# Block-sparse attention followed by a Fourier-mixing MLP: key sums read first, second weight by casting DMA, second-product pieces moved past the norm, exponentials and causal selects over two PSUM banks

## Chip, cores, metric

One core of one Trainium2 chip runs the whole program. The metric is device microseconds (us) of one execution, lower is better. Each experiment ran its kernel and the kernel before on the same chip in the same session, and a verdict uses the runs of the fast state alone. For a single core that state only tells runs within 1.5% of the fastest from slower ones, and it is judged within a session: a run that counts as fast in one session can count as slow in another.

## The reference

The inputs are q, k, v of shape (4, 8, 768, 64) and two weights, (512, 2048) and (2048, 512), all float32. The output is (4, 768, 512).

```python
# attention: 12 key blocks of 64; each query keeps its own block and the 3 best causal blocks
k_rep = k.reshape(B, H, 12, 64, D).mean(axis=3)
gate  = where(causal_block, q @ k_rep^T, -1e9);  top_idx = argsort(gate)[..., -3:]
attn  = softmax(mask(top_idx or own block, causal)(q k^T / 8)) @ v        # (4, 8, 768, 64)
x     = attn with the heads side by side                                 # (4, 768, 512)
# MLP
u   = x + real(fft(fft(x, axis=1), axis=2))
un  = (u - mean(u)) / sqrt(var(u) + 1e-6)                                 # over the 512 features
out = u + relu(un @ w1) @ w2
```

## The kernel before

The eight heads of a batch are four pairs, so there are 16 pairs. A pair goes through four stages in four consecutive slots: A (transposes of q and k, key sums), B (gate), D (scores, exponentials, causal selects), V (times v). The MLP of batch b runs between the attention of batch b+1, piece by piece: a list of generators is interleaved by the cost that each piece states. So a piece's place in the program, not its readiness, decides when TensorE comes to it: in the trace of this kernel the last fold (`fg`) of batch 3 is done at 265.7 us, and TensorE takes up its first matmul on the folds at 286.4 us, behind eight second-product pieces (279.5 to 286.4 us) that stand before it in the program. That is what "in order" means. Batch 0's attention has no MLP beside it, and the last MLP has no attention beside it.

Names used below: `tp` transposes, `kr` key sums, `gtp`/`g`/`gmp` gate matmul, its transpose and the resulting mask, `sc` scores, `ptl` exponentials, `av` attention output, `sd`, `zw`, `fg` folds of x by symmetry, `yp` and `mx` the two Fourier matmuls, `ha`/`hb` the first product (512 and 256 columns), `ch` the second product.

Stage A: ScalarE copies a bank of transposed keys, then VectorE sums it per block (four such banks a pair, two of them keys).

```python
for who in range(2):                       # 0: q, 1: k
    for g in range(2):
        ps = pst([128, 3, 128], f"tp_{hp}_{who}_{g}")
        ...  # three TensorE transposes
        if who == 0:
            nc.vector.tensor_copy(out=qt[:, cols], in_=flat)
        else:
            nc.scalar.copy(out=kI[0][0:64, cols], in_=flat[0:64])
            nc.scalar.copy(out=kI[1][0:64, cols], in_=flat[64:128])
            nc.vector.tensor_reduce(out=kr12[:, 6 * g:6 * g + 6], in_=..., op=add)
...
for e in range(2):                         # query copies, on GpSimd
    nc.gpsimd.tensor_scalar(out=qg[e][0:64, :], in0=qt[64 * e:64 * e + 64, :], ...)
```

Stage D: six PSUM banks of scores per head, one exponential each; the bank holding diagonal blocks gets a causal select on GpSimd.

```python
for bi, bank in enumerate(BANKS):          # 5 banks of 512 columns, 1 of 128
    for e in range(2):
        sp = pst([128, wid_bank], ..., tag="sc", bufs=3)      # 5 general banks + 3 of these
        ...  # matmuls
        nc.scalar.activation(out=pt[:, po:po + wid_bank], in_=sp, func=AF.Exp, scale=0.125)
        if ndiag:
            nc.gpsimd.affine_select(out=dg, in_=dg, ...)
```

Weights: sixteen loads of 0.5 MB into float32 staging (issued by SyncE), sixteen float32-to-float16 casts on GpSimd.

```python
W_LOAD = {1: ('fft', 0, 1, 2, 3), 3: (4, 5, 6, 7), 5: (8, 9, 10, 11), 7: (12, 13, 14, 15)}
W_CAST = {3: (0, 1, 2, 3), 5: (4, 5, 6, 7), 7: (8, 9, 10, 11), 9: (12, 13, 14, 15)}
def emit_weight_cast(c): nc.gpsimd.tensor_scalar(out=dst, in0=wst[c], ...)
```

MLP of batch b, with the 24 pieces (four matmuls, 0.86 us each) of the second product of batch b-1 as filler `w2(n)`:

```python
tt(fg..., ADD);  yield from w2(2)
tt(fg..., SUB);  yield from w2(1)
tt(fg..., SUB);  yield from w2(1)
tt(fg..., ADD);  yield from w2(4)
...  # yp: first Fourier matmul, copies
for hf in range(2):
    ...  # mx: second Fourier matmul, u, statistics
    yield from w2(4)
    ...  # normalise three row tiles, DMA-transpose them into unT
    yield from w2(2)
yield from w2(100)                         # what is left
...  # first product (ha, hb) from unT
```

The softmax here doesn't subtract the row's maximum and nothing guards it: scores larger than these inputs give would overflow.

## Time and profile before

| | before |
|---|---|
| time | 363.17 us, median of 3 (362.57 to 363.66) |
| profiled execution, span | 358.5 us |
| TensorE clock, mean over the span | 0.94 |

The table of busy time by stretches of 20 us. Each line gives the stretch, its length, then busy us and instructions for TensorE (PE), its weight loads (PEld), VectorE (DVE), ScalarE (ACT), GpSimd (POOL), then the granted TensorE clock, the mean DMA share, and GB/s.

```profile
core 0: us, PE busy (x) PEld busy (x) DVE busy (x) ACT busy (x) POOL busy (x), PEclk, DMA share, GB/s
20.00:40.00 20.00, 17.22 (x174) 11.97 (x169) 12.54 (x50) 15.62 (x36) 12.77 (x21) 0.91 1.11 236
40.00:60.00 20.00, 16.31 (x188) 11.75 (x186) 16.50 (x57) 15.32 (x34) 17.96 (x24) 0.91 1.23 234
60.00:80.00 20.00, 16.35 (x174) 11.58 (x173) 19.25 (x60) 13.84 (x31) 14.52 (x18) 0.91 1.11 237
80.00:100.00 20.00, 14.80 (x167) 10.21 (x166) 19.31 (x52) 11.31 (x27) 12.60 (x17) 0.85 0.88 169
100.00:120.00 20.00, 19.38 (x151) 11.86 (x151) 15.03 (x48) 11.40 (x24) 6.89 (x10) 0.73 0.59 101
...
200.00:220.00 20.00, 20.00 (x175) 12.54 (x173) 13.36 (x47) 12.50 (x26) 5.05 (x8) 1.00 0.16 12
...
300.00:320.00 20.00, 16.36 (x75) 7.84 (x74) 7.88 (x18) 2.84 (x5) 1.11 (x2) 0.83 0.28 73
```

From 120 to 300 us TensorE is 95 to 100% busy at full clock. From 20 to 100 us no engine is the limit alone; VectorE comes nearest at 60 to 100 and GpSimd at 40 to 60. A closer look, in stretches of 4 us, at the end of that stage:

```profile
84.00:88.00 4.00, 4.00 (x40) 3.24 (x38) 4.00 (x11) 3.31 (x7) 2.58 (x5) 1.00 1.51 203
88.00:92.00 4.00, 2.91 (x39) 2.17 (x37) 4.00 (x19) 3.86 (x10) 3.80 (x6) 1.00 0.37 74
92.00:96.00 4.00, 0.92 (x21) 0.81 (x21) 4.00 (x6) 0.00 (x0) 3.84 (x5) 0.73 0.60 61
96.00:100.00 4.00, 3.02 (x18) 1.42 (x18) 4.00 (x12) 0.37 (x1) 0.48 (x1) 0.50 0.90 132
100.00:104.00 4.00, 3.68 (x24) 3.04 (x24) 3.75 (x11) 1.65 (x4) 1.17 (x3) 0.50 0.99 204
104.00:108.00 4.00, 4.00 (x15) 1.54 (x14) 3.97 (x20) 3.90 (x8) 2.94 (x5) 0.50 0.41 80
```

At 92 to 96 us VectorE has no free moment and TensorE works 0.92 us; the clock is 0.50 from 93.9 us, for 17.1 us. What VectorE and GpSimd did there, from the timeline (start, length, engine, line, operation, output and inputs):

```profile
90.86 1.97 DVE L324 SCALAR_TENSOR_TENSOR gmp_1550<-gsb_1548,other_75 128x144 f16<-128x144 f32 x1
```

```profile
90.66 0.91 POOL L230 DMA_DIRECT2D v_all<-in_v_dram  x1
91.61 1.06 POOL L201 TENSOR_SCALAR w_sb<-wst_1220 128x1024 f16<-128x1024 f32 x1
```

`gmp` takes 1.97 us here and 0.30 elsewhere (23.93 and 33.59 us, for instance). It ends just after GpSimd's cast does.

In the view of waits (who waited for whom: us in total, times, longest), VectorE's key sums wait for ScalarE's copies of the same bank; the two lines add up to 15.5 us over the whole run:

```profile
DVE kr_1_78 L282 <- ACT kI_all L281: 10.2, 9, 2.2
...
DVE kr_0_77 L282 <- ACT kI_all L281: 5.3, 6, 1.9
```

The end of the run, from the timeline; the bracket gives idle time and what ended it. The last second-product pieces of batch 2 run out at 306.5 us:

```profile
305.59 1.03 PE L572 MATMUL ch_5_4621<-w_sb,hT_2_3_4147 128*128 128x512 f16 x4
...
307.48 0.38 PE L559 MATMUL ha_0_4644<-unT_4491,w_sb 128*128 128x512 f16 x1 [0.87 <-DVE u_3464 L576]
...
310.63 0.37 PE L560 MATMUL hb_0_4645<-unT_4491,w_sb 128*128 128x256 f16 x1 [2.77 <-DMA unT_4491<-x_3666]
...
310.80 0.63 PE L559 MATMUL ha_0_4644<-unT_4491,w_sb 128*128 128x512 f16 x1
...
311.44 0.63 PE L559 MATMUL ha_0_4644<-unT_4491,w_sb 128*128 128x512 f16 x1
```

TensorE stands still for 0.87 and 2.77 us and then needs 0.63 us for a matmul that takes 0.38 at full clock (the granted clock is 0.50 from 308.9 us, for 6.8 us).

### The profile page before, as it was taken

The numbers are of one execution on the slowest core, as the hardware profiler recorded it, in microseconds if no ns is written. First come the engines' busy times: TensorE is split into PE (matmuls) and PEld (weight loads), VectorE is DVE, ScalarE is ACT, GpSimd is POOL, SyncE is SP. The second block draws the span as 40 slices with busy tenths as digits, with TensorE's granted clock in tenths as the row PEclk, the third lists the DMA queues.
The fourth block names the chain that finished last, engine by engine and source line by source line (L and its number), as shares of the span: only waits on it lengthen the run. The fifth ranks groups of instructions, "written<-read, shape, count | busy, mean of one in ns | idle before, by whom it ended". The sixth has DMA issues, their size and how long they took to land.

```text
span 358.5 us, 7035 instructions
## 1 busy us (share of the span) xinstructions
PE 323.4 (90%) x2650; PEld 197.5 (55%) x2650; DVE 227.7 (64%) x690; ACT 175.8 (49%) x363; POOL 117.9 (33%) x174
## 2 busy tenths in 40 slices
PE   5678978699499999999899999999999999599995
PEld 2346656467355665656466665656565555256442
DVE  1564987999995765579857576499673167323121
ACT  1497767578264764647266854733634130034100
POOL 2574988686743410315332312141300002000000
PEclk9698989999758999999999999999999999789999
DMA  9999999989565350354923030013300003300012
GB/s 184 181 155 276 260 274 184 299 201 259 68 142 94 56 68 0 101 71 97 148 73 24 4 22 32 31 45 60 103 2 2 29 32 102 103 2 0 29 69 79
DMA packets 96154, 35.47 MB, mean 99 GB/s; under 512 B 89224, under 2 KB 89704, under 8 KB 96120
## 3 DMA queue, kind: packets, MB, share of 16 engines
q1 hardware_dynamic: 66296, 30.65, 34.2%
q0 software_dynamic: 25120, 3.18, 14.4%
q10 hardware_dynamic: 4704, 1.18, 2.1%
q8 instruction: 21, 0.34, 0.4%
q14 instruction: 13, 0.11, 0.1%
HBM read 28.71 MB, written 6.29 MB: 98 GB/s over the span
## 4 chain that ended last, share of the span: by engine, by line
PE 63%; DVE 19%; ACT 12%; DMA 3%; issue 2%; POOL 0%; SPq 0%; ACTq 0%; DVEq 0%; POOLq 0%
ACT kI_all L281 2%; DMA qn_103<-in_q_dram 2%; ACT kI_all L280 2%; DVE sd_596 L452 1%; DVE kr_0_77 L282 1%; PE warm L129 1%; PE ch_0_3470 L572 1%; PE ch_0_2295 L572 1%; PE ch_2_3773 L572 1%; DVE x_1358 L546 1%; PE ch_5_4931 L572 1%; PE ch_5_4621 L572 1%; PE ch_5_4081 L572 1%; PE ch_4_3981 L572 1%; PE ch_2_4874 L572 1%
## 5 line engine op out<-in xcount | busy, mean ns | idle before, releaser
L354 PEld LDWEIGHTS <-kI_all 76*128 76x128 f16 x416 | 33.2, 102 | 19.7 <-issue 4.4
L559 PEld LDWEIGHTS <-w_sb 128*128 128x128 f16 x256 | 25.6, 100 | 30.4 <-issue 4.3
L230 POOL DMA_DIRECT2D v_all<-in_v_dram x32 | 27.5, 861 | 30.0 <-PE av_0_1873 L386 4.8
L560 PEld LDWEIGHTS <-w_sb 128*128 128x128 f16 x256 | 25.4, 100 | 8.4 <-issue 4.9
L540 POOL TENSOR_SCALAR rstd_3_4493<-stat_3_4492 128x3 f32<-128x3 f32 x2 | 0.5, 234 | 46.8 <-DVE stat_3_4492 L537 46.8
L561 ACT ACTIVATE hT_3_0_4640<-ha_0_4644 128x512 f16<-128x512 f32 x1 | 0.6, 597 | 22.3 <-issue 22.3
L129 PE MATMUL warm<-warm_src 128*128 128x512 f16 x26 | 11.4, 438 | 0.0
L540 POOL TENSOR_SCALAR rstd_2_3705<-stat_2_3704 128x3 f32<-128x3 f32 x2 | 0.5, 235 | 18.5 <-DVE stat_2_3704 L537 18.5
L452 DVE TENSOR_TENSOR sd_596<-x_543 128x384 f16<-128x384 f16 x8 | 5.1, 654 | 0.1
L129 PEld LDWEIGHTS <-warm_src 128*128 128x128 f16 x26 | 2.8, 106 | 3.7 <-issue 3.4
L142 PE MATMUL warmps<-warm_src 128*128 128x512 f16 x8 | 3.6, 631 | 1.3 <-DVE kr_1_78 L149 1.3
L546 DVE TENSOR_SCALAR x_543<-u_1198,stat_0_1478,rstd_0_1479 128x512 f16<-128x512 f32 x6 | 4.5, 805 | 0.2 <-POOL rstd_0_1479 L542 0.2
L546 DVE TENSOR_SCALAR x_3666<-u_4394,stat_3_4492,rstd_3_4493 128x512 f16<-128x512 f32 x6 | 2.9, 543 | 2.6 <-POOL rstd_3_4493 L542 2.6
L365 POOL TENSOR_SCALAR_AFFINE_SELECT ptl_0_2318<-ptl_0_2318 128x512 f16<-128x512 f16 (+1 forms) x2 | 1.0, 520 | 10.7 <-ACT ptl_0_2318 L361 10.7
L546 DVE TENSOR_SCALAR x_1358<-u_2289,stat_1_2535,rstd_1_2536 128x512 f16<-128x512 f32 x6 | 3.8, 671 | 0.8 <-POOL rstd_1_2536 L542 0.8
L560 PE MATMUL hb_0_4645<-unT_4491,w_sb 128*128 128x256 f16 x4 | 1.6, 406 | 2.8 <-DMA unT_4491<-x_3666 2.8
L304 ACT COPY gts_1729<-gtp_1725 96x256 f32<-96x256 f32 x1 | 0.4, 368 | 7.4 <-PE gtp_1725 L301 7.4
L508 ACT CAST yg_0_4448<-yp_0_4441 128x386 f16<-128x386 f32 x1 | 0.6, 599 | 6.9 <-PE yp_0_4441 L497 6.9
L562 DVE TENSOR_SCALAR hT_3_0_4640<-hb_0_4645 128x256 f16<-128x256 f32 x1 | 0.4, 424 | 5.6 <-PE hb_0_4645 L560 5.6
L572 PEld LDWEIGHTS <-hT_3_1_4641 128*128 128x128 f16 x24 | 2.3, 98 | 2.8
L572 PEld LDWEIGHTS <-hT_3_2_4642 128*128 128x128 f16 x24 | 2.3, 98 | 2.8
L572 PEld LDWEIGHTS <-hT_3_3_4643 128*128 128x128 f16 x24 | 2.3, 98 | 2.8
(1765 smaller groups left out, 1100.2 us busy)
## 6 DMA issues: line engine op xcount, KB each, us to landing
v_all<-in_v_dram POOLq DMA_DIRECT2D x32, 96.0 KB, 4.5
out_dram<-u_1198 SPq DMA_DIRECT2D x6, 256.0 KB, 2.1
out_dram<-u_2289 SPq DMA_DIRECT2D x6, 256.0 KB
out_dram<-u_3464 SPq DMA_DIRECT2D x6, 256.0 KB, 2.1
out_dram<-u_4394 SPq DMA_DIRECT2D x6, 256.0 KB, 2.0
fs_sb<-c_FS SPq DMA_DIRECT2D x1, 582.0 KB, 5.2
wst_177<-in_moe_w_ch_dram SPq DMA_DIRECT2D x1, 512.0 KB, 7.0
wst_180<-in_moe_w_ch_dram SPq DMA_DIRECT2D x1, 512.0 KB
```

What stands on the lines that cost most here:

```text
L129: nc.tensor.matmul(wt, wsrc[:, 0:128], wsrc, start=True, stop=True)
L142: nc.tensor.matmul(wps, wsrc[:, 0:128], wsrc, start=True, stop=True)
L230: nc.gpsimd.dma_start(out=v16_t[e][hp][:, :, 0:64], in_=v[b, 2 * hp + e].rearrange("(jt p) d -> p jt d", p=128))
L280: nc.scalar.copy(out=kI[0][0:64, cols], in_=flat[0:64])
L281: nc.scalar.copy(out=kI[1][0:64, cols], in_=flat[64:128])
L282: nc.vector.tensor_reduce(out=kr12[:, 6 * g:6 * g + 6], in_=ps.rearrange("p a (x c) -> p a x c", x=2), axis=mybir.AxisListType.X, op=mybir ...
L354: nc.tensor.matmul(sp[:, co:co + (a1 - a0)], kI[e][0:76, 128 * jt:128 * (jt + 1)], qg[e][0:76, a0:a1], start=True, stop=True)
L452: nc.vector.tensor_tensor(out=sd[:, sgn, :, cols], in0=x_b[:, 0:3, cols], in1=x_b[:, 3:6, cols], op=op)
L546: nc.vector.tensor_scalar(out=un16[:, st, :], in0=u_b[:, st, :], scalar1=stat6[:, st, 0:1], scalar2=rstd6[:, st:st + 1], op0=SUB, op1=mybi ...
L559: nc.tensor.matmul(ha, w1s, unT[dt][:, 0:512], start=(dt == 0), stop=(dt == NDT - 1))
L560: nc.tensor.matmul(hb, w1s, unT[dt][:, 512:768], start=(dt == 0), stop=(dt == NDT - 1))
L572: nc.tensor.matmul(cps, hT[it][:, 128 * st:128 * (st + 1)], w2_sb[:, it, :], start=(it == 0), stop=(it == NIT - 1))
```

## The change

Six edits in one:

1. The key sum is issued ahead of the two copies (a branch that would take the sums to TensorE is present but switched off, `hp < 0`).
2. The second weight comes by four casting DMAs of 1 MB straight to float16, in slots 7 to 10. The first weight keeps staging and casts, its casts moved from slots 3 and 5 to 4 and 7.
3. Four of the 24 second-product pieces move from before the first Fourier matmul to after the norm.
4. Exponentials and selects cover two banks: three exponentials (1024, 1024, 640 columns) per head for six, one select (768) for two.
5. For that, score tiles take two sets of two banks, and the general PSUM pool falls from five banks to four.
6. Ten of twelve block maxima per pair; the first row tile needs none, as it has fewer than three causal blocks.

```diff
-    psump = ... bufs=5 ...
+    psump = ... bufs=4 ...
-    W_LOAD = {1: ('fft', 0, 1, 2, 3), 3: (4, 5, 6, 7), 5: (8, 9, 10, 11), 7: (12, 13, 14, 15)}
-    W_CAST = {3: (0, 1, 2, 3), 5: (4, 5, 6, 7), 7: (8, 9, 10, 11), 9: (12, 13, 14, 15)}
+    W_LOAD = {1: ('fft', 0, 1, 2, 3), 4: (4, 5, 6, 7), 7: (8,), 8: (9,), 9: (10,), 10: (11,)}
+    W_CAST = {4: (0, 1, 2, 3), 7: (4, 5, 6, 7)}
@@ emit_weight_load
+        if c >= 8:
+            it = 4 * (c - 8)
+            after(w2_sb[0:1, it, 0:1], attn_P[c - 2]["qt"][0:1, 0:1])     # a gate in time
+            nc.gpsimd.dma_start(out=w2_sb[:, it:it + 4, :], in_=moe_w_ch2[128 * it:128 * (it + 4), :]...)
+            return
@@ stage A
-                        nc.scalar.copy(out=kI[0][0:64, cols], in_=flat[0:64])
-                        nc.scalar.copy(out=kI[1][0:64, cols], in_=flat[64:128])
                         nc.vector.tensor_reduce(out=kr12[...], ...)
+                        nc.scalar.copy(out=put(kI[0][0:64]), in_=tp[0:64])
+                        nc.scalar.copy(out=put(kI[1][0:64]), in_=tp[64:128])
@@ stage B
-            for st in range(NST):
+            for st in range(1, NST):
                 for e in range(2):
                     nc.vector.max(out=mx8[:, st, e, :], in_=g4[:, st, e, 0:NB])
@@ stage D
-            for bi, bank in enumerate(BANKS):
+            for bi in range(0, len(BANKS), 2):
-                    sp = pst([128, wid_bank], ..., tag="sc", bufs=3)
+                    sp = pst([128, 1024], ..., tag="sc", bufs=2)
-                    nc.scalar.activation(out=pt[:, po:po + wid_bank], in_=sp, ...)
+                    nc.scalar.activation(out=pt[:, po:po + co], in_=sp[:, 0:co], ...)
@@ gen_mlp
-        yield from w2(2)      # after the first fold
+        yield from w2(1)
-        yield from w2(4)      # after the last fold
+        yield from w2(1)
... cut: mx8 and kr24 as fixed tiles, slices, warm-up tile
```

More of the change, by code (lines that the diff above doesn't have):

```diff
@@ L97 @@
     cpool = ctx.enter_context(tc.tile_pool(name="cst", bufs=1))
-    psump = ctx.enter_context(tc.tile_pool(name="psum", bufs=5, space=bass.MemoryType.PSUM))
+    psump = ctx.enter_context(tc.tile_pool(name="psum", bufs=4, space=bass.MemoryType.PSUM))
     apool = ctx.enter_context(tc.tile_pool(name="attn", bufs=2))
@@ L112 @@
     half24 = cpool.tile([128, 32], FP, tag="c_half", name="half24")
+    mx8_t = [cpool.tile([128, NST, 2, 8], FP, tag=f"mx8_{i}", name=f"mx8_{i}") for i in range(2)]
     kr16_t = [cpool.tile([128, 16], FP, tag=f"kr16_{i}", name=f"kr16_{i}") for i in range(2)]
+    kr24_t = [cpool.tile([128, 32], FP, tag=f"kr24_{i}", name=f"kr24_{i}") for i in range(2)]
     eps1 = cpool.tile([128, 1], FP, tag="c_eps1", name="eps1")
@@ L139, in emit_priority_consts @@
         nc.vector.memset(wsrc, 0.0)
-        wps = pst([128, 512], "warmps", tag="sc", bufs=3)
+        wps = pst([128, 512], "warmps")
         for i in range(8):
@@ L147, in emit_gate_consts @@
         nc.sync.dma_start(half24, dr["half24"].ap())
-        for t in kr16_t:
+        for t in mx8_t:
+            nc.vector.memset(t, -3e38)
+        for t in kr16_t + kr24_t:
             nc.vector.memset(t, 0.0)
@@ L177, in emit_weight_load @@
     def emit_weight_load(c):
+        if c >= 8:
+            it = 4 * (c - 8)
+            after(w2_sb[0:1, it, 0:1], attn_P[c - 2]["qt"][0:1, 0:1])
+            nc.gpsimd.dma_start(out=w2_sb[:, it:it + 4, :],
+                                in_=moe_w_ch2[128 * it:128 * (it + 4), :]
+                                .rearrange("(i p) l -> p i l", p=128))
+            return
         stg = bpool.tile([128, 1536], FP, tag=f"hT4_{c % 4}", name=f"wst_{c}")[:, 0:1024]
@@ L183, in emit_weight_load @@
             gate_on(stg[0:1, 0:1])
-        if c < 8:
-            dt, hf = divmod(c, 2)
-            nc.sync.dma_start(out=stg, in_=moe_w_ch1[128 * dt:128 * (dt + 1),
-                                                     1024 * hf:1024 * (hf + 1)])
-        else:
-            it = 2 * (c - 8)
-            nc.sync.dma_start(out=stg.rearrange("p (i l) -> p i l", i=2),
-                              in_=moe_w_ch2[128 * it:128 * (it + 2), :]
-                              .rearrange("(i p) l -> p i l", p=128))
-    def emit_weight_cast(c):
-        if c < 8:
-            dt, hf = divmod(c, 2)
-            dst = w1_sb[:, dt, 1024 * hf:1024 * (hf + 1)]
-        else:
-            it = 2 * (c - 8)
-            dst = w2_sb[:, it:it + 2, :].rearrange("p i l -> p (i l)")
+        dt, hf = divmod(c, 2)
+        nc.sync.dma_start(out=stg, in_=moe_w_ch1[128 * dt:128 * (dt + 1),
+                                                 1024 * hf:1024 * (hf + 1)])
+    def emit_weight_cast(c):
+        dt, hf = divmod(c, 2)
+        dst = w1_sb[:, dt, 1024 * hf:1024 * (hf + 1)]
         nc.gpsimd.tensor_scalar(out=dst, in0=wst[c], scalar1=1.0, scalar2=0.0,
                                 op0=mybir.AluOpType.mult, op1=mybir.AluOpType.add)
-    W_LOAD = {1: ('fft', 0, 1, 2, 3), 3: (4, 5, 6, 7), 5: (8, 9, 10, 11), 7: (12, 13, 14, 15)}
-    W_CAST = {3: (0, 1, 2, 3), 5: (4, 5, 6, 7), 7: (8, 9, 10, 11), 9: (12, 13, 14, 15)}
+    W_LOAD = {1: ('fft', 0, 1, 2, 3), 4: (4, 5, 6, 7), 7: (8,), 8: (9,), 9: (10,), 10: (11,)}
+    W_CAST = {4: (0, 1, 2, 3), 7: (4, 5, 6, 7)}
     x_tiles = {}
@@ L263, in stage_A @@
             kI = [kI_t[e][sl] for e in range(2)]
-            kr24 = apool.tile([128, 32], FP, tag="kr24", name=f"kr24_{hp}")
+            kr24 = kr24_t[hp % 2]
             kr12 = kr16_t[hp % 2]
             d["qt"], d["qg"], d["kI"], d["kr24"] = qt, qg, kI, kr24
+            pairs = hp < 0
+            krs = kr12.rearrange("p (o n) -> p o n", o=1)
             for who in range(2):
@@ L269, in stage_A @@
                 for g in range(2):
-                    ps = pst([128, 3, 128], f"tp_{hp}_{who}_{g}")
+                    ps = pst([128, 512], f"tp_{hp}_{who}_{g}")
+                    tp = ps[:, 0:384].rearrange("p (a c) -> p a c", a=3)
                     for i in range(3):
-                        st = 3 * g + i
-                        nc.tensor.transpose(ps[:, i, :],
-                                            src[:, st, :, :].rearrange("p h d -> p (h d)"), id32)
-                    flat = ps.rearrange("p a c -> p (a c)")
@@ L276, in stage_A, with put @@
-                    cols = slice(384 * g, 384 * (g + 1))
+                        nc.tensor.transpose(tp[:, i, :],
+                                            src[:, 3 * g + i, :, :].rearrange("p h d -> p (h d)"),
+                                            id32)
+                    def put(t):
+                        return t[:, 384 * g:384 * (g + 1)].rearrange("p (a c) -> p a c", a=3)
                     if who == 0:
-                        nc.vector.tensor_copy(out=qt[:, cols], in_=flat)
+                        nc.vector.tensor_copy(out=put(qt), in_=tp)
@@ L279, in stage_A @@
                     else:
-                        nc.scalar.copy(out=kI[0][0:64, cols], in_=flat[0:64])
-                        nc.scalar.copy(out=kI[1][0:64, cols], in_=flat[64:128])
-                        nc.vector.tensor_reduce(
-                            out=kr12[:, 6 * g:6 * g + 6],
-                            in_=ps.rearrange("p a (x c) -> p a x c", x=2),
-                            axis=mybir.AxisListType.X, op=mybir.AluOpType.add)
-                    yield 0.33
-            nc.vector.tensor_tensor(out=kr24.rearrange("p (e n) -> p e n", e=2),
-                                    in0=kr12.rearrange("p (o n) -> p o n", o=1)
-                                    .to_broadcast([128, 2, 16]),
-                                    in1=half24.rearrange("p (e n) -> p e n", e=2),
-                                    op=mybir.AluOpType.mult)
+                        if pairs and g == 1:
+                            for st in range(NST):
+                                nc.tensor.matmul(ps[:, 384 + 2 * st:386 + 2 * st],
+                                                 kn[:, st, :, :].rearrange("p h d -> p (h d)"),
+                                                 half24[:, 0:32:16], start=True, stop=True)
@@ new lines, in stage_A @@
+                        if pairs and g == 1:
+                            krs = ps[:, 384:400].rearrange("p (o n) -> p o n", o=1)
+                        elif not pairs:
+                            nc.vector.tensor_reduce(
+                                out=kr12[:, 6 * g:6 * g + 6],
+                                in_=tp.rearrange("p a (x c) -> p a x c", x=2),
+                                axis=mybir.AxisListType.X, op=mybir.AluOpType.add)
+                        nc.scalar.copy(out=put(kI[0][0:64]), in_=tp[0:64])
@@ L292, in stage_A @@
+                        nc.scalar.copy(out=put(kI[1][0:64]), in_=tp[64:128])
+                    yield 0.33
+            nc.vector.tensor_tensor(
+                out=kr24.rearrange("p (e n) -> p e n", e=2)[:, :, 0:NB],
+                in0=krs[:, :, 0:NB].to_broadcast([128, 2, NB]),
+                in1=half24.rearrange("p (e n) -> p e n", e=2)[:, :, 0:NB],
+                op=mybir.AluOpType.mult)
             for e in range(2):
@@ L316, in stage_B @@
             g4 = gsb.rearrange("p (s e n) -> p s e n", e=2, n=16)
-            mx8 = spool.tile([128, NST, 2, 8], FP, tag="mx8", name=f"mx8_{hp}", bufs=4)
-            for st in range(NST):
+            mx8 = mx8_t[hp % 2]
+            for st in range(1, NST):
                 for e in range(2):
@@ L344, in stage_D_scores @@
                                   bufs=2) for e in range(2)]
-            po = 0
-            for bi, bank in enumerate(BANKS):
-                wid_bank = sum(a1 - a0 for (_, a0, a1) in bank)
+            for bi in range(0, len(BANKS), 2):
                 for e in range(2):
                     pt = d["pt"][e]
-                    sp = pst([128, wid_bank], f"sc_{hp}_{e}_{bi}", tag="sc", bufs=3)
+                    sp = pst([128, 1024], f"sc_{hp}_{e}_{bi}", tag="sc", bufs=2)
+                    po = 512 * bi
                     co = 0
                     ndiag = 0
-                    for (jt, a0, a1) in bank:
+                    for (jt, a0, a1) in chain(*BANKS[bi:bi + 2]):
                         nc.tensor.matmul(sp[:, co:co + (a1 - a0)],
@@ L360, in stage_D_scores @@
                         co += a1 - a0
-                    nc.scalar.activation(out=pt[:, po:po + wid_bank], in_=sp, func=AF.Exp,
+                    nc.scalar.activation(out=pt[:, po:po + co], in_=sp[:, 0:co], func=AF.Exp,
                                          scale=0.125)
@@ L368, in stage_D_scores @@
                             channel_multiplier=-1)
-                po += wid_bank
-                yield 0.38
+                    yield 0.38
         def stage_D_av(hp):
```

## The prediction

> **What bounds it now.** The profile (span 358.5 us; runs 363.2) has two regimes, seen in busy time by stretches. From 120 to 300 us TensorE is busy 95 to 100% at clock 1.00: matmul-bound. From 20 to 100 us it is busy 15 to 17 of every 20 us and no engine alone is the limit: VectorE 19.3 of 20 at 60-100, GpSimd 18.0 at 40-60, ScalarE 14 to 15.6 at 20-80. The chain of waits there alternates between ScalarE (exponentials 0.49-0.60 us, kI copies 0.35-0.47) and VectorE. At 92-96 VectorE is the whole chain (gmp 1.97, three normalise steps 2.7 us), TensorE is busy 0.9 of 4 us, and its clock is then 0.50 until 108. At the end (timeline 306-316) TensorE idles 0.9 + 2.8 us for the last norm and transposes, then runs five us at half speed (631 against 379 ns).
>
> **What changes.**
> 1. Tail. Four 0.86 us pieces of the second product move past the norm. The last input of the final first product lands 12.6 us after the last mixing matmul (298.0 to 310.6). Mixing starts 3.45 us earlier; 12.1 us of product remain to cover it, so the idle falls below 1 us and the half-speed stretch (2.3 us lost) mostly goes. [...] Folds were ready at 265, used at 286: the earlier place costs nothing. Estimate: -5 us.
> 2. Second weight. Eight GpSimd casts (1.03-1.34 us, 9 us in all) become four casting DMAs (issue near 0.9 us, as the v loads' 0.86). VectorE is slowed beside GpSimd: a fold 1.1 against 0.34, gmp 1.97 against 0.30, a normalise step 0.9 against 0.54. [...] The slot of the fg folds keeps four casts, but pair 9's slot (92-96) loses all. Estimate: -3 us there and perhaps half of the 0.50-clock stretch (about 14 us of matmuls at half speed): -2 more.
> 3. Key sums first. VectorE waits 15.5 us in total for kI copies (view of waits), delaying the gate (gtp waits 2.0, 1.2, 3.0 us on kr). ScalarE will instead wait for the reduction (0.46). Estimate: -2 us.
> 4. Wide exponentials. From 512 (0.49) and 128 columns (0.17) the fixed part is 0.06 us; six fewer per pair save 0.4 us, selects 0.3 us of GpSimd, two fewer maxes 0.15 us of VectorE. Over eight slots: -2 us.
> 5. Cost: general PSUM buffers fall from five to four, and ScalarE starts only on two full banks: +1.5 us. Work saved beside a full TensorE gains nothing.
>
> Sum -12.5 us: **350.7 us**, 80% range 342 to 358. Chances: faster 0.81, within 2% 0.16, slower 0.03.
>
> **What would show it.** Last first product starts within 1 us of the last second product, at 379 ns. The first ha matmul (107 us now) comes 6 to 10 us earlier; kr no longer waits for kI. GpSimd busy falls from 118 to about 100 us, ScalarE from 176 to about 165. Clock at 92-108 well above 0.50. The mixed stage after that keeps its length.
>
> **What would make it wrong.** Four PSUM buffers starve TensorE in the mixed stage; a late VectorE reduction blocks ScalarE's exponentials; casting DMAs' descriptors are slow or collide with q/k loads; the clock halves elsewhere.

That the half-speed stretch would mostly go with the pause, and that fewer casts would free VectorE, was the author's estimate: the trace of before shows half speed from 308.9 us, where TensorE had worked 1.51 of the last 3.41 us, and a `gmp` of 1.97 us beside GpSimd against 0.30 elsewhere, and not the reason for either. -5, -3 and -2, -2, -2 and +1.5 make the -12.5 us, from 363.2 to 350.7. By "descriptors" the prediction and the expectations mean what a DMA issued by GpSimd costs it: 0.86 us on average for a load of v in the trace of before, 0.76 to 0.85 us for a casting DMA in that of the changed kernel.

## The result, and the profile after

| | before | after |
|---|---|---|
| time, median | 363.42 us (362.57 to 364.72, 4 runs) | 348.96 us (346.3 to 350.03, 4 runs) |
| ratio, 95% interval | | 0.9588 (0.9527 to 0.965) |
| profiled span | 358.5 us | 347.2 us |
| first `ha` of batch 0 starts | 106.9 us | 102.1 us |
| first `ch` of batch 2 starts | 279.5 us | 274.7 us |
| from there to the end | 79.0 us | 72.6 us |
| VectorE held up, 0 to 115 us | 8.5 us | 4.0 us |
| GpSimd busy, ScalarE busy | 117.9, 175.8 us | 106.3, 171.7 us |

A ratio is the mean time of one kernel's fast runs over that of the other's of the same rounds, so it is not quite the ratio of the medians. "Held up" is worked out: the busy time of five groups of VectorE instructions with both ends in SBUF (`sd`, `zw`, `fg`, `gmp`, the normalise step), less their count times the undisturbed length seen in the same traces (0.345, 0.551, 0.548, 0.30 and 0.53 us).

The three rows of starts split the span in three. The first stage became 4.8 us shorter, the last 6.4, and the middle kept its length (172.6 us in both). That makes up the 11.3 us between the two profiles. The medians differ by 14.5. All four runs of before in that session (362.57 to 364.72) counted as fast, but the profiled run of before took 360.3 us, and in the four later sessions this kernel ran from 355.6 to 366.4. Against the four runs of before that count as fast in the control's session (mean 359.7 us) the control's six runs of the changed kernel (mean 349.1) gain 10.6 us. So the gain lies between about 10.6 and 14.5 us, with the profiles' 11.3 inside. How it splits over the stages is known from that one pair of profiles alone.

Busy time of the changed kernel by stretches, as for before:

```profile
20.00:40.00 20.00, 17.11 (x162) 11.23 (x162) 14.69 (x57) 16.69 (x25) 15.89 (x20) 0.91 1.13 208
40.00:60.00 20.00, 17.52 (x201) 12.27 (x199) 16.36 (x43) 14.54 (x23) 13.54 (x16) 0.91 1.28 263
60.00:80.00 20.00, 17.36 (x152) 10.93 (x151) 16.61 (x56) 14.65 (x25) 12.16 (x16) 0.83 1.13 189
80.00:100.00 20.00, 13.22 (x164) 9.06 (x161) 19.23 (x57) 8.32 (x13) 10.50 (x14) 0.91 0.83 117
100.00:120.00 20.00, 18.68 (x157) 11.89 (x158) 11.87 (x37) 11.21 (x18) 6.13 (x8) 0.84 0.67 93
...
200.00:220.00 20.00, 20.00 (x186) 12.83 (x184) 13.52 (x43) 12.87 (x23) 4.39 (x6) 1.00 0.19 24
...
300.00:320.00 20.00, 20.00 (x122) 11.67 (x120) 6.22 (x14) 7.85 (x14) 0.00 (x0) 1.00 0.14 47
```

The stretch at 300 us is full now. The end, from the timeline: the last second-product pieces of batch 2 run straight into the first product, at 0.38 us a matmul, with no bracket of idle time.

```profile
298.78 2.97 PE L584 MATMUL ch<-w_sb,hT 128*128 128x512 f16 x13
...
301.59 0.38 PE L571 MATMUL ha<-unT,w_sb 128*128 128x512 f16 x1
...
301.95 0.38 PE L571 MATMUL ha<-unT,w_sb 128*128 128x512 f16 x1
```

The half-speed stretch has not gone, it has become shorter and moved (4 us stretches of the changed kernel):

```profile
88.00:92.00 4.00, 2.87 (x16) 1.94 (x15) 3.97 (x17) 1.73 (x3) 1.59 (x3) 0.68 0.61 127
92.00:96.00 4.00, 2.71 (x50) 2.20 (x49) 4.00 (x12) 1.35 (x3) 2.82 (x4) 0.89 1.10 170
96.00:100.00 4.00, 1.06 (x12) 0.47 (x11) 3.39 (x12) 1.83 (x5) 1.67 (x3) 0.96 1.48 196
100.00:104.00 4.00, 2.83 (x13) 1.34 (x14) 0.99 (x2) 1.02 (x1) 0.87 (x1) 0.50 0.77 85
104.00:108.00 4.00, 4.00 (x25) 2.68 (x23) 2.04 (x13) 1.95 (x3) 0.86 (x1) 0.69 0.00 0
```

Where VectorE's key sums waited for ScalarE's copies, ScalarE's copies now wait for the key sums. This is the view of waits for ScalarE:

```profile
ACT kI_all L298 <- DVE kr L294: 18.2, 9, 6.2
```

In both traces one of the two waits for the other at the bank that both read: VectorE 15.5 us before, ScalarE 18.2 us after. Why they do not read it at the same time, no run here shows. And these are sums over the whole run. Of the 18.2 us, 6.2 and 4.0 are ScalarE's first two waits, which end at 9.1 and 15.5 us; in the kernel before ScalarE idled 6.4 and 2.5 us at the same two places, for the transposes. From 20 us to the first `ha` VectorE waited 4.3 us for the copies before, and ScalarE waits 4.9 us for the sums after. Swapping the order turned the wait round; it did not take it away.

### The profile page after: what moved, and what is told of

The parts are those of the page before. It is cut to its first block, busy times and chain, and to the rows that moved or that the text cites. A ratio compares the mean times of both kernels' runs of the same rounds, so it can differ in the third digit from the quotient of the medians.

```text
span 347.2 us, 6862 instructions
## 1 busy us (share of the span) xinstructions
PE 319.0 (92%) x2650; PEld 194.7 (56%) x2650; DVE 224.2 (65%) x662; ACT 171.7 (49%) x267; POOL 106.3 (31%) x142
## 4 chain that ended last, share of the span: by engine, by line
PE 75%; DVE 9%; DMA 7%; ACT 6%; issue 1%; POOL 0%; SPq 0%; ACTq 0%; DVEq 0%; POOLq 0%
PE ch L584 23%; PE ha L571 16%; PE hb L572 8%; PE sc L367 7%; PE tp L276 5%; DMA kn<-in_k_dram 5%; PE av L398 4%; PE yp L509 2%; ACT ptl L374 2%; PE gtp L315 2%; PE mx L542 1%; DMA qn<-in_q_dram 1%; PE mx L540 1%; PE gt L349 1%; DVE qg L351 1%
## 5 line engine op out<-in xcount | busy, mean ns | idle before, releaser
L374 ACT ACTIVATE ptl<-sc 128x1024 f16<-128x1024 f32 (+1 forms) x96 | 85.4, 918 | 41.4 <-PE sc L367 38.5
L584 PE MATMUL ch<-w_sb,hT 128*128 128x512 f16 x384 | 91.0, 379 | 0.0
L571 PE MATMUL ha<-unT,w_sb 128*128 128x512 f16 x256 | 85.8, 384 | 0.6 <-DMA unT<-x 0.6
L572 PE MATMUL hb<-unT,w_sb 128*128 128x256 f16 x256 | 69.8, 274 | 0.1
L573 ACT ACTIVATE hT<-ha 128x512 f16<-128x512 f32 x64 | 38.2, 597 | 62.8 <-PE ha L571 41.4
L367 PE MATMUL sc<-qg,kI_all 76*128 76x128 f16 (+2 forms) x416 | 56.0, 260 | 9.1 <-DVE qg L351 5.0
L584 PEld LDWEIGHTS <-hT 128*128 128x128 f16 x384 | 35.4, 97 | 38.5 <-issue 1.8
L574 DVE TENSOR_SCALAR hT<-hb 128x256 f16<-128x256 f32 x64 | 27.1, 423 | 42.6 <-PE hb L572 42.5
L378 POOL TENSOR_SCALAR_AFFINE_SELECT ptl<-ptl 128x768 f16<-128x768 f16 x32 | 28.5, 890 | 71.2 <-ACT ptl L374 71.1
L367 PEld LDWEIGHTS <-kI_all 76*128 76x128 f16 x416 | 32.4, 101 | 25.9 <-issue 8.7
L307 POOL TENSOR_SCALAR qg<-qT 64x768 f16<-64x768 f32 x32 | 26.8, 838 | 18.2 <-DVE qT L284 16.8
L298 ACT CAST kI_all<-tp 64x384 f16<-64x384 f32 x32 | 15.0, 470 | 18.4 <-DVE kr L294 18.2
L284 DVE COPY qT<-tp 128x384 f32<-128x384 f32 x32 | 17.1, 547 | 5.2 <-PE tp L276 5.2
```

Source lines behind the costliest of these rows:

```text
L367: nc.tensor.matmul(sp[:, co:co + (a1 - a0)], kI[e][0:76, 128 * jt:128 * (jt + 1)], qg[e][0:76, a0:a1], start=True, stop=True)
L374: nc.scalar.activation(out=pt[:, po:po + co], in_=sp[:, 0:co], func=AF.Exp, scale=0.125)
L378: nc.gpsimd.affine_select(out=dg, in_=dg, pattern=[[0, ndiag], [1, 128]], compare_op=mybir.AluOpType.is_ge, fill=zero_fill, base=0, channe ...
L571: nc.tensor.matmul(ha, w1s, unT[dt][:, 0:512], start=(dt == 0), stop=(dt == NDT - 1))
L572: nc.tensor.matmul(hb, w1s, unT[dt][:, 512:768], start=(dt == 0), stop=(dt == NDT - 1))
L573: nc.scalar.activation(out=hT[it][:, 0:512], in_=ha, func=AF.Relu)
```

## The experiments

Three theories stood after the first look.

- T1: the parts are independent. Each one alone, on the kernel before, gives its share.
- T2: the parts need one another. Before the norm of batch 0, VectorE, GpSimd and ScalarE pass one chain around, and taking one wait away only shows the next.
- T3: the first stage is mostly the TensorE clock, which falls to 0.50 after stretches of little work (in the kernel before at 93.9 us, when TensorE had worked 1.52 of the last 3.41 us) and eats or returns gains by chance.

Tables of all runs come first, the single experiments after. "First ha", "end" and "held up" are read from each run's profile as above; "half speed" is the time at clock 0.50 before 120 us, from the clock records of the trace. The column "before, same session" is the median of all runs of before, fast and slow, while the ratio uses fast runs. Profiled runs are single ones, so differences of one or two us there mean little.

| run | median us | before, same session | ratio (95% interval) | first ha | end | held up | half speed |
|---|---|---|---|---|---|---|---|
| before | 363.42 | | | 106.9 | 79.0 | 8.5 | 34.1 |
| changed | 348.96 | 363.42 | 0.9588 (0.9527, 0.965) | 102.1 | 72.6 | 4.0 | 30.7 |
| changed again (control) | 349.3 | 363.43 | 0.9608 (0.9558, 0.9657) | 102.5 | 72.5 | 5.6 | 23.9 |
| b_tail: part 3 alone | 358.33 | 362.23 | 0.9966 (0.9812, 1.0121) | 112.0 (slow) | 73.0 | 6.6 (slow) | 44.4 (slow) |
| b_order: part 1 alone | 364.41 | 362.23 | 1.0154 (1.001, 1.0297) | 108.7 | 79.0 | 8.4 | 27.3 |
| b_cast: part 2 alone | 362.85 | 362.23 | 1.0116 (0.9991, 1.024) | 104.3 | 77.6 | 3.0 | 34.1 |
| b_wide: parts 4, 5 alone | 360.36 | 362.23 | 1.006 (0.9966, 1.0154) | 108.1 | 79.6 | 8.7 | 34.1 |
| a_notail: all but part 3 | 356.48 | 361.67 | 0.9884 (0.9831, 0.9937) | 104.7 | 77.7 | 4.1 | 20.5 |
| a_oldorder: all but part 1 | 350.67 | 361.67 | 0.9707 (0.9658, 0.9756) | 102.0 | 72.6 | 6.6 | 20.5 |
| a_nocast: all but part 2 | 354.98 | 361.67 | 0.9842 (0.9802, 0.9882) | 107.9 | 73.0 | 10.2 | 30.7 |
| a_nowide: all but 4, 5 | 354.03 | 361.67 | 0.9804 (0.9767, 0.984) | 105.6 | 72.5 | 5.2 | 30.7 |
| i_w1dma: a further step | 344.17 | 363.43 | 0.9461 (0.9416, 0.9505) | 96.4 | 72.8 | 5.2 | 17.1 |
| i_pairs: a further step | 363.29 | 363.43 | 1.0003 (0.9947, 1.0059) | 114.7 | 72.6 | 7.2 | 38.3 |
| a_spread: loads moved | 346.47 | 359.85 | 0.9673 (0.9626, 0.9719) | 99.2 | 73.1 | 6.8 | 20.5 |

All outputs were correct. The kernel before is the noisier of the two, so ratios of different sessions carry its noise with them; its median moved from 359.85 to 363.43 between sessions. Where a ratio and a median disagree, the text says so.

The ratios of different sessions do not share one yardstick. In the session of the four b_ runs only two of eleven runs of before counted as fast (355.70 and 361.01, mean 358.4), so all four ratios there hang on those two runs and share their error; each is unclear. In the session of the control the ratio of 0.9608 works out to a mean of about 363.3 us for before, so it counts runs that the list calls slow; on the four runs listed as fast it would be 0.9705. The a_ runs have no control in their own session and on their own chip either. For sums over runs the kernels are therefore put on two common yardsticks, worked out from the listed runs: the mean of each kernel's fast runs over that of the fast runs of before in its session, or the same with all runs.

| | b_tail | b_order | b_cast | b_wide | control | a_notail | a_oldorder | a_nocast | a_nowide |
|---|---|---|---|---|---|---|---|---|---|
| listed fast runs | 0.9966 | 1.0154 | 1.0116 | 1.0060 | 0.9705 | 0.9884 | 0.9707 | 0.9842 | 0.9804 |
| all runs | 0.9905 | 1.0060 | 1.0007 | 0.9952 | 0.9627 | 0.9857 | 0.9680 | 0.9812 | 0.9777 |

### One part alone

**b_tail**: only part 3.

```diff
-        yield from w2(2)
+        yield from w2(1)
-        yield from w2(4)
+        yield from w2(1)
```

> Kernel before with only the second-product pieces moved past the norm. My theory: the gain at the end is this part's alone. From the first second-product matmul of batch 2 to the end of the span takes 79.0 us before and 72.6 us after the whole change; this kernel shows 72.6 and is 6 to 6.5 us faster than before, no gap before the last first product, clock 1.00 there. Rival: the earlier parts free engines that the tail needs, so this part alone gives clearly less, 3 us or so.

The end took 73.0 us against 79.0, as my theory has it. This holds although the profiled run was slow, because the end lies after everything that made it slow. The median is only 3.9 us below before, the fast runs only 1.2 us (0.3%, unclear). The first stage of this run began its first product at 112.0 us, 5 us late, so the timed gain is muddied by the first stage. The end is settled; whether the moved pieces also cost time in the first stage is not, as the only profile is a slow one.

**b_order**: only part 1.

```diff
-    nc.scalar.copy(...); nc.scalar.copy(...); nc.vector.tensor_reduce(...)
+    nc.vector.tensor_reduce(...); nc.scalar.copy(...); nc.scalar.copy(...)
```

> Kernel before with only the key sum (VectorE) moved ahead of the two kI copies (ScalarE). My theory: -2 us, all of it before the first ha matmul (106.9 us), because the gate sums come earlier. Rival: ScalarE then queues behind a late VectorE reduction (in the changed kernel it waits 18.2 us in total for kr, up to 6.2 us once), so it is a wash or a loss of up to 2 us.

The rival was nearer, but the verdict is unclear: 1.5% slower against the two fast runs of before, 0.6% slower with all runs. The gate matmul of pair 5 starts 4.6 us earlier than before (53.8 against 58.4 us), so the sums did come sooner. Then this happened, in the timeline of that kernel:

```profile
53.02 1.04 POOL L201 TENSOR_SCALAR w_sb<-wst 128x1024 f16<-128x1024 f32 x1
...
54.01 0.87 POOL L230 DMA_DIRECT2D v_all<-in_v_dram  x1
...
54.91 1.06 POOL L201 TENSOR_SCALAR w_sb<-wst 128x1024 f16<-128x1024 f32 x1
54.98 3.10 DVE L452 TENSOR_TENSOR sd<-x 128x384 f16<-128x384 f16 x2
...
55.91 0.87 POOL L230 DMA_DIRECT2D v_all<-in_v_dram  x1
...
56.81 1.06 POOL L201 TENSOR_SCALAR w_sb<-wst 128x1024 f16<-128x1024 f32 x1
...
58.72 2.43 PE L354 MATMUL sc<-qg,kI_all 76*128 76x128 f16 x14 [3.06 <-DVE qg L337]
```

The two folds take 3.10 us (0.35 each undisturbed) while GpSimd runs a cast, issues a DMA and runs a second cast back to back. TensorE waits 3.06 us for the mask row that follows on VectorE, its clock halves at 57.1 us for 6.8 us (the same matmul, `warm`, takes 0.39 us at 54.31 and 0.64 us at 61.58), and by pair 7 the lead is gone (83.1 against 82.6 us).

**b_cast**: only part 2.

```diff
-    W_LOAD = {1: ('fft', 0, 1, 2, 3), 3: (4, 5, 6, 7), 5: (8, 9, 10, 11), 7: (12, 13, 14, 15)}
-    W_CAST = {3: (0, 1, 2, 3), 5: (4, 5, 6, 7), 7: (8, 9, 10, 11), 9: (12, 13, 14, 15)}
+    W_LOAD = {1: ('fft', 0, 1, 2, 3), 4: (4, 5, 6, 7), 7: (8,), 8: (9,), 9: (10,), 10: (11,)}
+    W_CAST = {4: (0, 1, 2, 3), 7: (4, 5, 6, 7)}
+    (second weight by nc.gpsimd.dma_start into w2_sb)
```

> Kernel before with only the second weight loaded by casting DMA and the load and cast slots of the change. My theory: -3 to -5 us, in the stretch before the first ha matmul, as VectorE is held up less beside GpSimd; GpSimd busy falls from 118 to about 107 us; the long VectorE instructions at 90-96 us (1.97 us gmp, 0.9 us normalise steps) are short. Rival: the casts were never on the path, since TensorE is in order and waits on other things there; then within 1 us of before.

The mechanism came, the time did not. VectorE was held up 3.0 us in place of 8.5, the `gmp` of that stage took 0.29 us, and the first `ha` came at 104.3 in place of 106.9 us. One normalise step of three still took 1.67 us, and GpSimd's busy time fell to 112.8 us, not to 107. The median did not move (362.85 against 362.23, unclear). The trace shows where it went: the pause before the first product still comes, and the clock is then 0.50 from 96.9 to 114.0 us, over the first product itself.

```profile
100.00:104.00 4.00, 3.53 (x20) 2.02 (x21) 3.67 (x10) 3.38 (x8) 3.30 (x6) 0.50 1.00 160
104.00:108.00 4.00, 2.17 (x5) 0.46 (x4) 2.58 (x15) 1.89 (x4) 2.91 (x5) 0.50 0.70 105
108.00:112.00 4.00, 3.87 (x16) 2.45 (x17) 0.76 (x2) 2.02 (x4) 0.00 (x0) 0.50 0.62 105
112.00:116.00 4.00, 4.00 (x52) 2.94 (x51) 1.79 (x6) 1.33 (x4) 0.87 (x1) 0.75 0.41 91
```

From the first `ha` to the first `ch` of batch 0 takes 36.2 us here and 32.4 before. The 2.6 us of lead were paid back there, as T3 has it, in this one run.

**b_wide**: only parts 4 and 5.

```diff
-    psump bufs=5; sp = pst([128, wid_bank], tag="sc", bufs=3); one Exp per bank; selects of 512 and 256
+    psump bufs=4; sp = pst([128, 1024], tag="sc", bufs=2);   one Exp per two banks; one select of 768
```

> Kernel before with only the two-bank exponentials and selects, which brings four general PSUM buffers in place of five. My theory: a net of 0 to -2 us: ScalarE busy falls by 3 to 5 us, but TensorE waits more for buffers and for two full banks. Rival: this is the main source of the early gain, -4 us or more; other rival: the lost buffer costs more than it gives, +1 us or more.

By the medians 1.9 us faster, on the fast runs 0.6% slower (about 2 us), unclear: neither the theory's 0 to -2 us nor the second rival's +1 us is excluded, and the first rival's -4 us is not seen. ScalarE's busy time fell from 175.8 to 170.6 us, as expected. What the lost PSUM buffer costs by itself was not tried.

Added up, the four parts alone give -3.0 us by the medians (-3.9 + 2.2 + 0.6 - 1.9), against -14.5 for the whole; with all runs 0.8% faster against 3.7% for the control; on the listed fast runs 3.0% slower against 2.9% faster. No single part's time is established, but the sum falls short of the whole by 3.0 to 5.9 points on either yardstick. T1 falls.

### All but one part

**a_notail**: the changed kernel with `w2(2)` and `w2(4)` again.

```diff
-        yield from w2(1)      # after the first fold
+        yield from w2(2)
-        yield from w2(1)      # after the last fold
+        yield from w2(4)
```

> Changed kernel with the second-product pieces put back ahead of the norm. My theory: the end is worth 6.4 us whatever stands before it, so the ratio to before goes from 0.959 to about 0.977 (355 us), with the gap and the half-speed stretch back before the last first product. Rival: moving the pieces also shifted the attention against batch 0's mixing and cost time there (the part alone gained only 3.9 us in the median), then the loss is about 4 us only.

Slower by 7.2 us than the control's median, which was taken on another chip; by 1.8 points on the fast runs and 2.3 with all runs. The end is 77.7 us against 72.5, with a half-speed stretch of one 3.4 us step there, not two as before. The end is thus worth 5 to 6.4 us. The rival expected a loss clearly smaller than that, about 4 us; 1.8 to 2.3 points, about 6.5 to 8.3 us, speak against it. They do not exclude a small cost.

**a_oldorder**: the changed kernel with the copies first.

```diff
-    tensor_reduce; copy; copy
+    copy; copy; tensor_reduce
```

> Changed kernel with the kI copies ahead of the key sum again. Alone, the key sum first cost 1.5% (0.1 to 3.0). Theory A (interaction): with wide exponentials and fewer casts it gains, so this kernel is 2 to 4 us slower than the changed one. Theory B: the order is harmful or neutral in every company, so this kernel is as fast or up to 4 us faster than the changed one (ratio to before 0.959 or below).

Slower by 1.4 us than the control's median, by 0.5 points with all runs and by nothing on the fast runs (0.9707 against 0.9705), and the profiled spans are equal (347.3 and 347.2). Theory A's 2 to 4 us are not shown; theory B is not excluded. In the company of the other parts the new order gains 0 to 2 us, which is within the noise.

**a_nocast**: the changed kernel with staging and sixteen casts in the old slots.

```diff
-    W_CAST = {4: (0, 1, 2, 3), 7: (4, 5, 6, 7)}           (second weight by casting DMA)
+    W_CAST = {3: (0, 1, 2, 3), 5: (4, 5, 6, 7), 7: (8, 9, 10, 11), 9: (12, 13, 14, 15)}
```

> Changed kernel with the second weight through staging and GpSimd casts again, in the old slots. Alone, the casting DMA gained nothing (ratio 1.012, interval 0.999 to 1.024). Theory A (interaction): GpSimd's casts hold up VectorE and the wide selects more once the other waits are gone, so this kernel is 3 to 6 us slower than the changed one (ratio about 0.97 to 0.975). Theory B: no effect in any company, ratio 0.959.

Slower by 5.7 us than the control's median, by 1.4 points on the fast runs and 1.9 with all runs. VectorE is held up 10.2 us against 4.0 and 5.6, and the first `ha` comes at 107.9 against 102.1. Theory A holds: the same part for which no gain could be shown alone is worth 5 to 7 us here.

**a_nowide**: the changed kernel with one-bank exponentials and five general buffers.

```diff
-    psump bufs=4; sp = pst([128, 1024], tag="sc", bufs=2)
+    psump bufs=5; sp = pst([128, wid_bank], tag="sc", bufs=3)
```

> Changed kernel with one-bank exponentials and selects, five general PSUM buffers and three score buffers again. Theory A: the wide exponentials are what makes the key sum first bearable, as ScalarE has fewer instructions behind it and TensorE one score bank more: this kernel is 4 to 8 us slower than the changed one (ratio about 0.97 to 0.98). Theory B: their worth is what it was alone, 0 to 2 us (ratio about 0.96 to 0.965).

Slower by 4.7 us than the control's median, by 1.0 point on the fast runs and 1.5 with all runs: the lower end of A, or a little below it.

Each part taken away costs 7.2, 1.4, 5.7 and 4.7 us, 19 us in all by the medians, more than the whole gives; the four alone gave 3.0 in all. On the fast runs the four costs add up to 4.2 points against 2.9 for the whole, with all runs to 6.2 against 3.7. Parts whose sum falls short alone and overshoots in company need one another. This is what T2 expects, and it holds on either yardstick. The sums are rough, as each term carries an uncertainty of one to five us and terms of one session share the error of its kernel before. Which pair of parts carries the interaction was not tried.

T3 is not settled. Half speed in one profile does not foretell a median: the changed kernel had 30.7 us of it in one profile and 23.9 in the other with equal medians, and a_notail had 20.5 with a median 7.2 us longer. But the record lists the mean clock of every run, and span times (1 - clock) gives the clock lost in it. Over the 45 runs of before in the later sessions it goes with the span (correlation 0.73). Its mean is 20 to 22 us for before, 19 to 24 us for each part alone, 12 to 16 us with one part left out, and 11 to 12 us for the whole. So no part alone won back lost clock worth speaking of (19.4 us at the least, against 19.9 for before in that session), and the whole won back about 9 us: the interaction shows in the clock too, and not only by chance. Whether the clock is its cause or only follows from TensorE's pauses, no run here separates; T2 and T3 may be two views of one thing.

### Further steps

**after_again** is the changed kernel as a control.

> The changed kernel itself, as a control on the chip of the two further steps. Ratio to before 0.955 to 0.965; first ha matmul at 100 to 104 us in the trace; the stretch from the first second-product matmul of batch 2 to the end 72.6 us.

It came out as expected (0.9608, first `ha` at 102.5 us, end 72.5 us), so the result stands on two sessions.

**i_w1dma**: the first weight by casting DMA too; no GpSimd cast is left.

```diff
-    W_LOAD = {1: ('fft', 0, 1, 2, 3), 4: (4, 5, 6, 7), 7: (8,), ...}
-    W_CAST = {4: (0, 1, 2, 3), 7: (4, 5, 6, 7)}
+    W_LOAD = {1: ('fft',), 3: (0,), 4: (1,), 5: (2,), 6: (3,), 7: (8,), ...}
+    W_CAST = {}
+        if c < 4:
+            after(w1_sb[0:1, c, 0:1], attn_P[c + 2]["qt"][0:1, 0:1])
+            nc.gpsimd.dma_start(out=w1_sb[:, c, :], in_=moe_w_ch1[128 * c:128 * (c + 1), :])
+            return
```

> Changed kernel with the first weight loaded by casting DMA too, so no GpSimd cast at all is left. My theory (GpSimd's casts hold up VectorE in the first 100 us): the excess of VectorE's folds, gmp and normalise steps over their undisturbed length falls from 4.0 us to about 2, and the kernel is 1 to 4 us faster than the changed one. Rival: VectorE is held up by selects, query copies and descriptor writing as much as by casts, or four more descriptor jobs of 1 MB collide with the q, k and v loads: within 1 us, or slower.

Faster than the changed kernel by 5.1 us (344.17 against 349.3 in the same session), the best of all. But the reason I gave missed: VectorE was held up 5.2 us, not 2. Its own trace shows by what: 4.6 of the 5.2 us are the `gmp` of nine pairs, and the three longest (1.67, 1.75 and 1.75 us for 0.30) each begin under a causal select of GpSimd and end just after the query copy that follows it. So the rival was right about the selects and query copies, though not about the time. The gain is real and its cause was another one, at least in part. In the changed kernel the chain of waits (start, length, what) holds one long DMA:

```profile
29.67 12.74 DMA kn<-in_k_dram
```

It is the load of the keys of pair 4. SyncE issued it behind the burst of the Fourier constants and the first four weight loads of slot 1, and the key transposes of that pair start on it, with a wait, at 42.54 us:

```profile
42.54 0.87 PE L276 MATMUL tp<-id,kn 128*128 128x128 f32 x3 [0.48 <-DMA kn<-in_k_dram]
```

**i_pairs**: the switched-off branch switched on for pairs 0 to 8.

```diff
-            pairs = hp < 0
+            pairs = hp < 9
```

> Changed kernel with the dead branch switched on for pairs 0 to 8: the key sums come from six small TensorE matmuls in place of two VectorE reductions per pair. If VectorE is the limit in the first 100 us, this takes 0.9 us per pair off it and off ScalarE's wait for kr (15 us before 104 us): 2 to 5 us faster than the changed kernel. If TensorE, at half clock and in order, is the limit there, the extra weight loads (six per pair) cost as much as they save: within 1 us or slower.

A loss of 14 us against the control; 12.2 of the 13.9 us between the profiles come before the first `ha` (114.7 against 102.5). The added matmuls have two columns but each needs its own weight load, and the trace shows each of the six of a pair as two (108 in nine pairs):

```profile
L288 PEld LDWEIGHTS tp<-half,kn x108: 190/192/338, 9.0 to 106.3; 128*128 128x128 f32 x108
L288 PE MATMUL tp<-half,kn x108: 169/251/353, 9.2 to 106.3; 128*128 128x2 f32 x108
```

Twelve weight loads of 0.19 us are 2.3 us of TensorE's weight path per pair, in program order between the transposes and the scores. The chain of waits holds this line for 1.24 us in most pairs and 2.35 us in one. VectorE's 0.9 us were cheaper.

**a_spread**: the first weight's loads spread, its casts kept. This was to tell the two causes of i_w1dma apart.

```diff
-    W_LOAD = {1: ('fft', 0, 1, 2, 3), 4: (4, 5, 6, 7), ...}
+    W_LOAD = {1: ('fft',), 2: (0, 1), 3: (2, 3), 4: (4, 5, 6, 7), ...}
```

> Changed kernel with the same staging and the same eight GpSimd casts of the first weight, but its first four 0.5 MB loads no longer issued in one burst in slot 1: two in slot 2, two in slot 3. In the trace of the changed kernel the transposes of pair 4 wait until 42 us for its keys, whose load was issued at 29.9 us behind that burst; slot 3 to 4 of the gate matmul then takes 12.1 us, against 8.5 in the kernel without first-weight casts. If the burst is what the first weight's casting DMA took away, this kernel gains 3 us or more over the changed one (ratio to before about 0.95) and that slot falls to about 9 us. If it was the casts on GpSimd, it stays at 0.96 and the slot at 11 to 12 us.

The slot fell from 11.8 us (34.9 to 46.7, the gate matmuls of pairs 3 and 4 in the changed kernel) to 8.7 (35.2 to 43.9), and the first `ha` from 102.1 to 99.2 us. The median is 346.47, with all six runs from 346.21 to 347.44, against 347.1 to 350.91 for the control. The ratio, 0.967, shows little of the gain: 0.3 points on the fast runs and 0.2 with all runs, about 1 us, as the kernel before ran faster in that session (359.85 against 363.43). So the slot fell as foretold, and the 3 us in time were not shown (1 to 2.8 us). I read it as: the burst is shown in the trace to cost that slot 3 us, the first `ha` came 2.9 us earlier, about half of what i_w1dma gained there (5.7 to 6.1 us), and the other half lies with the casts or with the rest of the load schedule. That half stays open.

## Why the prediction was right

- **The time.** 350.7 us predicted, 348.96 measured, within 342 to 358. This is partly luck. The sum took the parts as independent, and they are not (T1 fell). In the profiles a first stage that gave less than predicted (4.8 us for about 7.5) was made up in part by an end that gave more (6.4 for 5).
- **Tail, -5 us.** Right in mechanism and a little small: the end went from 79.0 to 72.6 us, and it is 72.5 to 73.1 in every kernel that has the part and 77.6 to 79.6 in every one without. The gap went entirely; I had left up to 1 us of it.
- **Second weight, -3 and -2 us.** Right in size within the whole (5.7 us by the medians when taken away), and in mechanism: VectorE held up 8.5 to 4.0 us. What I did not see is that alone no gain would show. I costed the parts as if they added, and they do not. The sum was near the mark because all parts were there.
- **Key sums first, -2 us.** This is the weak step. The prediction said that ScalarE "will instead wait for the reduction (0.46)". The waits are 18.2 us in total; 10.2 of them are the start-up, and one of 2.7 us ends at 95.6 us, where VectorE does two updates of u and their statistics first. The 15.5 us that the step was to save were a sum over the whole run; only 5.6 us of them lie before the first `ha`, and the prediction itself says that work saved beside a full TensorE gains nothing (the middle stage kept its 172.6 us). Alone its median was 2.2 us longer (unclear), in company it gives 0 to 2 us.
- **Wide exponentials, -2 us, and +1.5 us for the PSUM buffer.** A net of -0.5 was predicted; alone it is -1.9 by the medians (unclear), in company -4.7. The cost of the buffer was not measured by itself; the middle stage kept its length.
- **First ha 6 to 10 us earlier.** 4.8 in the profile and 4.4 in the control's, short of the range.
- **Clock at 92 to 108 well above 0.50.** Half right. The long stretch at half speed, 17.1 us from 93.9, became 3.4 and 6.8 us, and at 100 to 104 us the clock is 0.50 still. Over the first 120 us the half-speed time fell from 34.1 to 30.7 and, in the control, 23.9 us.
- **GpSimd "about 100", ScalarE "about 165".** Measured 106.3 and 171.7. Both were sums done carelessly: the prediction's own parts give about 107 (9 us of casts and 5 of selects less, about 3.5 of issues more) and 169.5 (16 pairs of 0.4 us).

What stays open: which pair of parts interacts, whether the clock causes or follows that, the second half of i_w1dma's gain, and what each part gives alone.

## What to carry to other kernels

Where several engines pass a chain around and none is full, cost the parts of a change together and test them both alone and left out: here, by the medians, the parts alone gave 3 us and the whole 14.5. Keep a control in the session of each group of runs, and look at how many runs of the kernel before a ratio stands on. When a wait is summed over the whole run, count only what lies where the main engine is not full. Filler work belongs behind the longest wait of the last round, where nothing else can fill it; count the wait and the filler, as here, where 5 us were foretold and 6.4 came. After removing casts from an engine, look at when the loads are issued as well: here a burst of weight loads ahead of the next pair's keys cost 3 us in one slot.

## What the traces show of the clock and of VectorE beside GpSimd

- In the kernel before TensorE was at half clock for 34.1 of the first 120 us and for 6.8 us more from 308.9 us. Busy time in 2 us stretches times the lost clock gives, as an estimate from that trace, 14 us of 358.5 in the first 120 us alone, 4%. The half-speed stretches of that trace and of the changed kernel's, leaving out the last microseconds of each run, last 3.4, 6.8 or 17.1 us.
- TensorE had worked 1.52 and 1.51 us of the last 3.41 us when the clock halved at 93.9 and 308.9 us, and 2.56 us when it halved at 68.9 us in the changed kernel (busy times of the trace). The longest pause of TensorE in the trace of the kernel before was 3.0 us. So the clock halved after partly busy stretches too; below which share of busy time that happens, no run here shows.
- VectorE's wait reached across several GpSimd instructions in a row: 1.97 us for a 0.30 us instruction across a DMA issue and a 1.06 us cast (before), and 3.10 us for two folds of 0.35 across two casts and the DMA issue between (b_order). What makes it wait, no run here shows.
- A casting DMA of 1 MB took GpSimd 0.76 to 0.85 us of issue in the changed kernel, against two casts of 1.03 to 1.34 us for the same weights in the kernel before.
